# Gated linear recurrence and a two-layer network in one hand-ordered kernel: inputs loaded per unit, weights issued between them, old state added on the vector engine, output matmuls after the first silus

## The chip, the core and the metric

The kernel runs on one core of a Trainium2 chip. The core has a matrix engine (TensorE, here PE; PEld is its weight load), a vector engine (VectorE, DVE), an activation engine (ScalarE, ACT), a general engine (GpSimd, POOL), and SyncE (SP), which here only issues transfers. Sixteen DMA engines move the data. The metric is the device time of one execution in microseconds (µs), as the median of several runs.

## What is computed

A recurrence over 768 positions for 4 batches and 8 heads of 48 channels, followed by two matrix products with a silu between them:

```python
f = 1.0 / (1.0 + np.exp(-f_logit))
for t in range(S):
    state = f[:, :, t, :, None] * state + np.einsum('bhd,bhe->bhde', k[:, :, t], v[:, :, t])
    y[:, :, t] = np.einsum('bhd,bhde->bhe', q[:, :, t], state)
x = y.transpose(0, 2, 1, 3).reshape(B * S, H * D)      # 3072 x 384
h = x @ w_in                                            # 384 x 2048
out = (h * (1.0 / (1.0 + np.exp(-h)))) @ w_out          # 2048 x 384
```

The inputs q, k, v and f_logit are float32, 4.7 MB each; the weights are 3.1 MB each in float32 and are used in bfloat16.

## The kernel before

**Tiles and stages.** Positions are cut into 6 chunks of 128. A *unit* is one chunk of one batch (128 positions, 8 heads, 48 channels: 128x384), and a *half-chunk* `m` is two units, `m.0` and `m.1` (one chunk, two batches). There are 12 half-chunks and 24 units. Half-chunks m and m + 2 hold the same two batches, one chunk on, so the state goes from m to m + 2.

For each half-chunk the inputs `f`, `k`, `q`, `v` are loaded (`load`, SP), 128x768 float32 each. `logs` (ACT) makes log(1 + exp(-f)) in two instructions, `f_ld` and `lf`. Then for each unit:

- `cumsum` (cs, PE) sums the logs along the positions by a triangular matrix; `inverse` (ia) and `forward` (a) on ACT take their exponentials; `totals` and `decay_all` (al) give the decay of the whole chunk.
- `scale_k` (ki, POOL) and `scale_q` (qg, DVE) multiply k and q by them; `values` (vb, POOL, for half-chunk 1 on ACT) casts v.
- `transposes` (T, `t_ps`, PE) turns qg and ki, `transposed` (qk, DVE) copies them out of PSUM, `scores` (A, `a_ps`, PE) multiplies them, `masked` (am, `atm`, DVE) keeps the causal part in two instructions.
- `outputs` (Y, `y_ps`, PE) multiplies by v and, from half-chunk 2 on, adds the old state times q; `output_copy` (yc, DVE), `turn` (X, `x_ps`, PE) and `turned` (xT, DVE) make the network's input.
- `update` (D, `d_ps`, PE), in half-chunks 0 to 9, forms the new state; from half-chunk 2 on its first matmul multiplies the old state by the identity, so that it is summed in PSUM (L334). `state` (st, DVE) multiplies it by the decay.

For each half-chunk the network follows: eight steps I (`mlp_in`, six matmuls of 128x256 each, into `h_ps`), each with a silu S on ACT (`silu`, 128x512, into `hT`), then for each of the two batches four steps O (`mlp_out`, four matmuls of 128x384 each, into `o_ps`), a copy and a store (`result`, ACT, queue of ACT).

**What sets the order.** The order is written out by the program itself, before anything runs. `Plan` holds every step as a task with an engine, an assumed duration, needs, a rank and pools of buffers. `Plan.run` plays them through and notes when each would start; `emit` then issues the instructions in that order, and every engine works through its own part in exactly this order. `allowed` adds gates: steps I and O are not mixed except where the mode turns, ACT's table for exp and its table for silu are kept apart, and a step that opens an accumulator is held back while silus are pending. Until I0 starts, PE's waiting is filled with matmuls of zeros (`warm`, `w_ps`).

**Transfers.** Loads are issued on SP in the order f, k, q, v of half-chunk 0, then of 1. The weights are cast on the way, so they are issued on POOL, in eight pieces (four of `w_in` with 512 columns, four of `w_out` with four row blocks), all at once after ki of unit 1.1 (task `weights`). The loads of half-chunk 2 and later stand on SP behind a tiny transfer out of the sixth weight piece (`behind`, L477), so that they don't overtake the weights. The pool `ld` has four buffers for each input. In the built program all transfers of SP and ACT use eight landing counters in turn, in the order of issue, and one that takes a counter first waits for the last transfer on it.

Of the kernel before, what the change touches and what calls it, by code (L numbers as in the profile page):

```python
# [17 lines left out]
class Plan:  # L18
# [30 lines left out]
    def run(self, filler=None, until=None):  # L49
# [8 lines left out]
        self.silus = self.exps = turned = 0  # L58
        while left:
# [45 lines left out]
            if e == "PE" and kind in "IO":  # L105
                self.mode = kind
                if kind == "I" and t["name"].endswith(".0"):
                    self.silus += self.per_half
            if kind == "S":
                self.silus -= 1  # L110
# [17 lines left out]
    def allowed(self, cand, fronts, free):  # L128
# [4 lines left out]
        if kind in "IO" and t["engine"] == "PE":  # L133
            if kind == self.mode:
                return True
            now = [c for c in fronts.get("PE", ()) if c[2]["name"][0] == self.mode and c[0] <= start + 0.7]
            pending = self.mode == "I" and self.silus
            return not now and not pending and not (kind == "I" and self.exps)
        if t["opens"] > 0 and self.mode == "I" and self.silus:
            return False  # L140
        if t["table"] == "exp" and not t["opens"] and self.mode == "I" and self.silus:
            return False
        return True

# [6 lines left out]
def kernel(  # L151
# [24 lines left out]
    ld = ctx.enter_context(tc.tile_pool(name="ld", bufs=4))  # L176
# [9 lines left out]
    def load(m, name):  # L186

        g, b0 = m // 2, m % 2 * HB
        t = ld.tile([C, HB, H, D], F32, name=f"{name}_ld")
        loaded[m, name] = t  # L190
        src = SRC[name].rearrange("b h s d -> s (b h) d")[g * C:(g + 1) * C, b0 * H:(b0 + HB) * H]
        nc.sync.dma_start(out=t.rearrange("p b h d -> p (b h) d"), in_=src)  # L192
# [35 lines left out]
    def logs(m):  # L228
        act_table("exp")
        f = loaded[m, "f"]  # L230
        nc.scalar.activation(f, f, AF.Exp, scale=-1.0)  # L231
        nc.scalar.activation(lf[m % 4][:, :, :, 0:D], f, AF.Ln, bias=1.0)
# [17 lines left out]
    def scale_k(m, j):  # L250
        nc.gpsimd.tensor_mul(ki[m % 4][:, j, :, 0:D], loaded[m, "k"][:, j], ias[m, j])  # L251

    def scale_q(m, j):
        nc.vector.tensor_mul(qg[m % 4][:, j, :, 0:D], loaded[m, "q"][:, j], aas[m, j])  # L254

    def values(m, j):
        nc.gpsimd.tensor_copy(vb[m % 4][:, j], loaded[m, "v"][:, j])  # L257

    def values_act(m, j):
        nc.scalar.copy(vb[m % 4][:, j], loaded[m, "v"][:, j])  # L260
# [69 lines left out]
    def update(m, j):  # L330
        b = m % 2 * HB + j
        d_ps = yps.tile([128, NP, 2 * D], F32, name="d_ps", tag="yd")
        if m >= 2:
            nc.tensor.matmul(d_ps, ident, st[b], start=True, stop=False, skip_group_check=True)  # L334
        for p in range(NP):
            nc.tensor.matmul(d_ps[:, p, :], ki[m % 4][:, j, 2 * p:2 * p + 2, :], vb[m % 4][:, j, 2 * p:2 * p + 2],
                             start=(m < 2 and p == 0), stop=(p == NP - 1), skip_group_check=True)
        d[m, j] = d_ps

    def state(m, j):  # L340
        b = m % 2 * HB + j
        for r in range(2):
            lo = 64 * r
            nc.vector.tensor_mul(st[b][lo:lo + D, :, r * D:(r + 1) * D],  # L344
                                 d[m, j][lo:lo + D, :, r * D:(r + 1) * D],
# [56 lines left out]
    def loads(m):  # L402
        for name in "fkqv":
            needs = []
            if m >= 4:
                o = m - 4
                if name == "f":
                    needs = [f"L{o}"]
                else:
                    needs = [U({"k": "ki", "q": "qg", "v": "vb"}[name], o, j) for j in range(HB)]  # L410
            transfer(f"{name}{m}", 2.15 + 1.7 * (name + str(m) == "f0"), do(load, m, name), needs)
# [3 lines left out]
    for n in range(0, d_ff, 512):  # L415
        transfer(f"wi{n}", 2.05 + 1.0 * (n == 0), None, [])
# [5 lines left out]
    for m in range(NH):  # L422
        g = m // 2
        add(f"L{m}", "ACT", 1.7, do(logs, m), [f"f{m}"] + ([U("cs", m - 4, j) for j in range(HB)] + [f"al{m - 4}"] if m >= 4 else []),
            rank=m * 10 + 5, table="exp")
        add(f"al{m}", "PE", 0.2, do(totals, m), [f"L{m}"], rank=m * 10 + 9, takes="yd", opens=1)
# [97 lines left out]
```

## Time and profile before

| | |
|---|---|
| median of 4 runs | 211.31 µs (211.16 to 212.63) |
| the profiled execution | 211.16 µs, its span 209.4 µs, mean granted PE clock 0.975 |
| PE busy | 189.2 µs (90%), of it `h_ps` 70.2, `o_ps` 67.8, zeros 12.2 |
| ACT, DVE, POOL busy | 127.0, 99.4, 45.1 µs |
| loads on SP | 48 of 384 KB, 6.4 to 6.7 µs from issue to landing |
| weight pieces on POOL | 8 of 384 KB, `w_in` 7.6 and `w_out` 13.1 µs to landing |
| stores on ACT's queue | 24 of 192 KB, 3.4 µs to landing |

The span goes from the first to the last instruction; what lies around it belongs to the device time too. Where parts of a profile are quoted, a line of a group names line, engine, operation, output and inputs, sizes and count, then busy time and the mean of one instruction in ns. The chain of waits is followed back from the last instruction: each piece is what the next one waited for. Digits are tenths in 40 equal slices of the span. The groups that the steps below use most are these:

```profile
L353 PE MATMUL h_ps<-xT,w_in_sb 128*128 128x256 bf16 x576 | 70.2, 276 | 4.4 <-ACT hT L362 2.7
L368 PE MATMUL o_ps<-w_out_sb,hT 128*128 128x384 bf16 x384 | 67.8, 326 | 0.0
L297 DVE TENSOR_TENSOR atm<-a_ps,triu 128x512 bf16<-128x512 f32 x48 | 30.9, 686 | 4.5 <-PE a_ps L290 3.5
L251 POOL TENSOR_TENSOR ki<-k_ld,ia 128x384 bf16<-128x384 f32 x24 | 24.7, 1043 | 92.8 <-ACT ia L243 92.7
L254 DVE TENSOR_TENSOR qg<-q_ld,a 128x384 bf16<-128x384 f32 x24 | 19.1, 806 | 56.7 <-ACT a L248 49.7
L317 DVE CAST y<-y_ps 128x384 bf16<-128x384 f32 x24 | 13.3, 556 | 10.1 <-PE y_ps L310 9.7
L231 ACT ACTIVATE f_ld<-f_ld 128x768 f32<-128x768 f32 x12 | 10.1, 843 | 11.3 <-DMA f_ld<-in_f_logit_dram 7.0
L344 DVE TENSOR_TENSOR st<-d_ps,al 48x192 bf16<-48x192 f32 x40 | 14.0, 350 | 0.3
```

### The profile page before, as it was taken

Reading aid. Unit: us, or ns where it says so; the run is one execution under the profiler, and the core shown is the slowest. Engines: PE = TensorE matmul, PEld = TensorE weight load, DVE = VectorE, ACT = ScalarE, POOL = GpSimd, SP = SyncE. Lnnn points to the kernel's source line nnn. Section 1 sums busy time; section 2 is a strip of 40 time slices with the busy share of each in tenths; the row PEclk is TensorE's granted clock in tenths of the full one; section 3 lists DMA queues with packets and bytes.
Section 4 is the critical chain, followed back from the end, with each engine's and each line's share of the span. In section 5 each row is a group of like instructions: output and inputs, shape, how many; then the busy total and the mean of one; then the engine's idle time right before and its main releaser. Section 6 shows DMA issues by size and latency. Waiting matters only on the chain.

```text
span 209.4 us, 4687 instructions
## 1 busy us (share of the span) xinstructions
PE 189.2 (90%) x1957; PEld 139.6 (67%) x1957; DVE 99.4 (47%) x198; ACT 127.0 (61%) x220; POOL 45.1 (22%) x66
## 2 busy tenths in 40 slices
PE   7876899996389979959998999999999999999992
PEld 3544588663368658746677886678976778986651
DVE  3288840028348438302899712888307897200000
ACT  3534469471824986898957679817796227894111
POOL 4319600042401043004514101430006300000000
PEclk9997999999759999999999999999999999999999
DMA  7998999999999999999999800931001110000222
GB/s 133 187 187 123 167 198 202 193 246 211 216 191 181 186 203 226 189 166 187 242 180 248 129 3 5 258 83 41 0 0 41 38 49 29 3 0 3 75 75 75
DMA packets 106293, 27.04 MB, mean 129 GB/s; under 512 B 99616, under 2 KB 106272, under 8 KB 106272
## 3 DMA queue, kind: packets, MB, share of 16 engines
q1 hardware_dynamic: 99104, 18.88, 58.2%
q0 software_dynamic: 3712, 3.15, 9.8%
q10 hardware_dynamic: 3456, 4.72, 7.0%
q8 instruction: 15, 0.25, 0.5%
q14 instruction: 6, 0.05, 0.1%
HBM read 25.17 MB, written 4.72 MB: 143 GB/s over the span
## 4 chain that ended last, share of the span: by engine, by line
PE 63%; DMA 13%; ACT 7%; SPq 5%; DVE 5%; POOL 3%; issue 2%; ACTq 0%; DVEq 0%
PE h_ps L353 25%; PE o_ps L368 22%; DMA w_out_sb<-in_moe_w_out_dram 6%; SPq L192 5%; PE t_ps L278 4%; DMA k_ld<-in_k_dram 4%; DMA q_ld<-in_q_dram 3%; PE a_ps L290 3%; ACT L224 2%; PE y_ps L306 2%; PE y_ps L310 2%; ACT f_ld L231 2%; POOL w_in_sb L213 2%; PE cs L238 1%; PE x_ps L323 1%
## 5 line engine op out<-in xcount | busy, mean ns | idle before, releaser
L353 PE MATMUL h_ps<-xT,w_in_sb 128*128 128x256 bf16 x576 | 70.2, 276 | 4.4 <-ACT hT L362 2.7
L362 ACT ACTIVATE hT<-h_ps 128x512 bf16<-128x512 f32 x96 | 56.6, 597 | 24.0 <-PE h_ps L353 20.8
L368 PE MATMUL o_ps<-w_out_sb,hT 128*128 128x384 bf16 x384 | 67.8, 326 | 0.0
L353 PEld LDWEIGHTS <-w_in_sb 128*128 128x128 bf16 x576 | 54.8, 99 | 12.8 <-issue 4.0
L368 PEld LDWEIGHTS <-hT 128*128 128x128 bf16 x384 | 36.4, 98 | 21.8
L254 DVE TENSOR_TENSOR qg<-q_ld,a 128x384 bf16<-128x384 f32 x24 | 19.1, 806 | 56.7 <-ACT a L248 49.7
L251 POOL TENSOR_TENSOR ki<-k_ld,ia 128x384 bf16<-128x384 f32 x24 | 24.7, 1043 | 92.8 <-ACT ia L243 92.7
L297 DVE TENSOR_TENSOR atm<-a_ps,triu 128x512 bf16<-128x512 f32 x48 | 30.9, 686 | 4.5 <-PE a_ps L290 3.5
L374 ACT COPY o_sb<-o_ps 128x384 f32<-128x384 f32 x24 | 11.5, 478 | 30.3 <-PE o_ps L368 30.2
L224 ACT ACT_TABLE_LOAD x14 | 18.0, 1283 | 2.1 <-ACT o_sb L374 1.2
L283 DVE COPY qk<-t_ps 128x1024 bf16<-128x1024 bf16 x24 | 16.4, 684 | 5.1 <-PE t_ps L278 5.1
L317 DVE CAST y<-y_ps 128x384 bf16<-128x384 f32 x24 | 13.3, 556 | 10.1 <-PE y_ps L310 9.7
L257 POOL CAST vb<-v_ld 128x384 bf16<-128x384 f32 x22 | 11.9, 569 | 25.7 <-DMA v_ld<-in_v_dram 20.9
L231 ACT ACTIVATE f_ld<-f_ld 128x768 f32<-128x768 f32 x12 | 10.1, 843 | 11.3 <-DMA f_ld<-in_f_logit_dram 7.0
L243 ACT ACTIVATE ia<-cs 128x384 f32<-128x384 f32 x24 | 11.8, 492 | 5.3 <-PE cs L238 3.9
L344 DVE TENSOR_TENSOR st<-d_ps,al 48x192 bf16<-48x192 f32 x40 | 14.0, 350 | 0.3
L381 PE MATMUL w_ps<-zeros 128*128 128x384 bf16 x53 | 12.2, 380 | 1.1 <-DVE zeros L483 1.1
L310 PE MATMUL y_ps<-vb,atm 128*128 128x48 bf16 x192 | 11.9, 185 | 1.5 <-DVE atm L297 1.0
L310 PEld LDWEIGHTS <-atm 128*128 128x128 bf16 x192 | 10.0, 97 | 4.0 <-DVE atm L297 2.1
L248 ACT ACTIVATE a<-cs 128x384 f32<-128x384 f32 x24 | 11.8, 491 | 0.0
L278 PE MATMUL t_ps<-ident,qg 128*128 128x128 bf16 x96 | 9.8, 227 | 1.5 <-DVE qg L254 1.5
L306 PE MATMUL y_ps<-st,qk 128*128 128x96 bf16 x80 | 10.0, 206 | 1.1 <-DVE xT L328 0.7
(37 smaller groups left out, 134.8 us busy)
## 6 DMA issues: line engine op xcount, KB each, us to landing
f_ld<-in_f_logit_dram SPq DMA_DIRECT2D x12, 384.0 KB, 6.5
k_ld<-in_k_dram SPq DMA_DIRECT2D x12, 384.0 KB, 6.4
q_ld<-in_q_dram SPq DMA_DIRECT2D x12, 384.0 KB, 6.7
v_ld<-in_v_dram SPq DMA_DIRECT2D x12, 384.0 KB, 6.7
out_dram<-o_sb ACTq DMA_DIRECT2D x24, 192.0 KB, 3.4
w_in_sb<-in_moe_w_in_dram POOLq DMA_DIRECT2D x4, 384.0 KB, 7.6
w_out_sb<-in_moe_w_out_dram POOLq DMA_DIRECT2D x4, 384.0 KB, 13.1
behind<-w_out_sb SPq DMA_DIRECT2D x1, 0.1 KB, 4.2
```

Of the source, the lines that this page charges most:

```text
L224: nc.scalar.preload_act_table_set(tables[name])
L231: nc.scalar.activation(f, f, AF.Exp, scale=-1.0)
L251: nc.gpsimd.tensor_mul(ki[m % 4][:, j, :, 0:D], loaded[m, "k"][:, j], ias[m, j])
L254: nc.vector.tensor_mul(qg[m % 4][:, j, :, 0:D], loaded[m, "q"][:, j], aas[m, j])
L278: nc.tensor.transpose(t[:, i, p, :], src[m % 4][:, j, 2 * p:2 * p + 2, :], ident)
L283: nc.vector.tensor_copy(qkT[m, j], t_ps[m, j])
L297: nc.vector.tensor_mul(atm[m, j][:, r], att[m, j][:, r], triu[:, None, :].to_broadcast([C, NP, C]))
L306: nc.tensor.matmul(y_ps[:, 2 * p:2 * p + 2, :], qkT[m, j][:, 0, p, :], st[b][:, p, :], start=not opened, stop=False, skip_group_check=True)
L310: nc.tensor.matmul(y_ps[:, 2 * p + r, :], atm[m, j][:, r, p, :], vb[m % 4][:, j, 2 * p + r, :], start=not opened, stop=True, skip_group_ch ...
L353: nc.tensor.matmul(h_ps[:, i], w_in_sb[:, kk, (n + i) * 128:(n + i + 1) * 128], xT[m][:, kk].rearrange("p b c -> p (b c)"), start=(kk == 0 ...
L362: nc.scalar.activation(hT[m][:, n:n + 2, :], hs[m, n], AF.Silu)
L368: nc.tensor.matmul(os[m, j], hT[m][:, i, j * C:(j + 1) * C], w_out_sb[:, i, :], start=(i == 0), stop=(i == NT - 1))
```

## The change

Four things are changed together.

1. **Loads per unit.** Each load takes one unit (128x384, 192 KB) instead of a half-chunk; the order is f, k, q, v of unit m.0, then of m.1. The pool has eight buffers of half the size. The logs on ACT are made per unit as well, and a buffer comes free when one unit has used it.
2. **Weights between the loads.** The first weight piece is issued on POOL after vb of unit 0.1, the other seven after ki of unit 1.0, each a task of its own. `behind` needs the last piece's issue and the load of v of unit 1.1.
3. **Old state on DVE.** The matmul with the identity goes; from half-chunk 2 on, `state` first adds PSUM and the old state into a new tile `sd` (float32) and multiplies from there.
4. **Order of I, O and exp.** A step O needs the silus of its own four row blocks instead of all sixteen. PE may turn from I to O when all steps I of the half-chunk are issued, without its silus being done; exp work waits whenever silus are pending.

Assumed durations and ranks in the plan follow. The order that `Plan` writes out is therefore another one throughout.

```diff
@@ Plan.run @@
                 if kind == "I" and t["name"].endswith(".0"):
                     self.silus += self.per_half
+                    self.ins += self.per_half
+                self.ins -= kind == "I"
...
@@ Plan.allowed @@
-            now = [c for c in fronts.get("PE", ()) if c[2]["name"][0] == self.mode and c[0] <= start + 0.7]
-            pending = self.mode == "I" and self.silus
-            return not now and not pending and not (kind == "I" and self.exps)
-        if t["opens"] > 0 and self.mode == "I" and self.silus:
-            return False
-        if t["table"] == "exp" and not t["opens"] and self.mode == "I" and self.silus:
+            now = [c for c in fronts.get("PE", ()) if c[2]["name"][0] == self.mode and c[0] <= start + self.patience]
+            return not now and not (self.mode == "I" and self.ins) and not (kind == "I" and self.exps)
+        if (t["opens"] > 0 or t["table"] == "exp" and not t["opens"]) and self.silus:
             return False
...
-    ld = ctx.enter_context(tc.tile_pool(name="ld", bufs=4))
+    ld = ctx.enter_context(tc.tile_pool(name="ld", bufs=8))
...
-    def load(m, name):
+    def load(m, j, name):
...
-        t = ld.tile([C, HB, H, D], F32, name=f"{name}_ld")
+        t = ld.tile([C, H, D], F32, name=f"{name}_ld")
...
-    def logs(m):
+    def logs(m, j):
         act_table("exp")
-        f = loaded[m, "f"]
+        f = loaded[m, j, "f"]
         nc.scalar.activation(f, f, AF.Exp, scale=-1.0)
-        nc.scalar.activation(lf[m % 4][:, :, :, 0:D], f, AF.Ln, bias=1.0)
+        nc.scalar.activation(lf[m % 4][:, j, :, 0:D], f, AF.Ln, bias=1.0)
...
     def update(m, j):
-        b = m % 2 * HB + j
         d_ps = yps.tile([128, NP, 2 * D], F32, name="d_ps", tag="yd")
-        if m >= 2:
-            nc.tensor.matmul(d_ps, ident, st[b], start=True, stop=False, skip_group_check=True)
...
     def state(m, j):
         b = m % 2 * HB + j
+        src = d[m, j]
+        if m >= 2:
+            src = wk.tile([128, NP, 2 * D], F32, name="sd")
+            nc.vector.tensor_add(src, d[m, j], st[b])
...
-                                 d[m, j][lo:lo + D, :, r * D:(r + 1) * D],
+                                 src[lo:lo + D, :, r * D:(r + 1) * D],
...
     def loads(m):
-        for name in "fkqv":
...
+        for j in range(HB):
+            for name in "fkqv":
+                user = U({"f": "L", "k": "ki", "q": "qg", "v": "vb"}[name], m - 4, j)
+                first = (m, j, name) == (0, 0, "f")
+                transfer(U(name, m, j), 1.07 + 1.7 * first, do(load, m, j, name), [user] if m >= 4 else [])
...
                 add(f"O{m}.{j}.{n}", "PE", 0.655, do(mlp_out, m, j, n),
-                    [f"S{m}.{NT - 2}", f"wo{n}"] + ([f"O{m}.{j}.{n - 4}"] if n else []),
+                    [f"S{m}.{n + 2}", f"wo{n}"] + ([f"O{m}.{j}.{n - 4}"] if n else []),
...
-    add("weights", "POOL", 6.5, weights, [U("ki", 1, 1)], rank=-10)
+    pieces = [(load_w_in, n) for n in range(0, d_ff, 512)] + [(load_w_out, n) for n in range(0, NT, 4)]
+    before = U("vb", 0, 1)
+    for i, (fn, n) in enumerate(pieces):
+        if i == 1:
+            before = U("ki", 1, 0)
+        add(f"weights{i}", "POOL", 0.85, do(fn, n), [before], rank=-10 if i else 2.5)
+        before = f"weights{i}"
+
+
+    add("behind", "SP", 0.1, lambda: nc.sync.dma_start(out=behind, in_=w_out_sb[0:1, 4, 0:64]), [before, U("v", 1, 1)])
```

## The prediction

> **What bounds the kernel now.** I read the slices of the page first, then busy time by stage, then the chain of waits, then the DMA queues in short stretches. Times inside a run are µs from the span's start. The slices:
>
> ```profile
> PE   7876899996389979959998999999999999999992
> PEclk9997999999759999999999999999999999999999
> DMA  7998999999999999999999800931001110000222
> ```
>
> PE is the bound, but not evenly: DMA is full until about 115 µs, and PE has its holes only before that. The stages cut at I0 (23.3, first `h_ps` matmul of half-chunk 0), O0 (36.1), the end of O1 (47.7) and I2 (59.0) give their size; the columns are the stretch, its length, and the busy time of each engine:
>
> ```profile
> 23.30:36.10 12.80, 12.28 (x134) 10.64 (x135) 4.91 (x12) 8.74 (x15) 1.05 (x2) 1.00 1.25 194
> 36.10:47.70 11.60, 11.60 (x85) 6.98 (x82) 1.23 (x2) 6.81 (x13) 2.74 (x4) 1.00 1.16 221
> 47.70:59.00 11.30, 5.43 (x75) 3.79 (x75) 7.32 (x16) 5.16 (x9) 3.62 (x5) 0.84 1.15 209
> 59.00:76.00 17.00, 16.22 (x161) 11.99 (x160) 8.03 (x17) 10.76 (x17) 1.46 (x3) 0.90 1.27 187
> 76.00:95.00 19.00, 15.39 (x181) 12.83 (x178) 8.53 (x16) 15.39 (x25) 4.18 (x7) 1.00 1.23 195
> 95.00:112.00 17.00, 16.33 (x191) 11.17 (x190) 12.36 (x22) 12.71 (x25) 6.24 (x8) 1.00 1.23 211
> 112.00:206.00 94.00, 93.64 (x988) 71.50 (x985) 43.22 (x83) 56.97 (x102) 13.22 (x16) 1.00 0.24 56
> ```
>
> PE idles 5.9 µs at 47.7:59.0, then 0.8 + 3.6 + 0.7 = 5.1 up to 112, and 0.4 after it. So the end is the start of I0, plus PE's work, plus these holes: whatever moves I0 moves the end, unless a hole takes it up. The hole before I2 is the input of half-chunk 3, behind a store that waits on ACT (chain of waits):
>
> ```profile
> 44.19 7.83 DMA k_ld<-in_k_dram
> 52.10 0.34 ACTq L376
> 52.49 0.85 ACT f_ld L231
> ```
>
> What starts I0 is the first weight piece, issued on POOL at 18.1 and used at 23.3:
>
> ```profile
> 18.11 3.24 POOL L213 DMA_DIRECT2D w_in_sb<-in_moe_w_in_dram  x4
> 23.32 0.83 PE L353 MATMUL h_ps<-xT,w_in_sb 128*128 128x256 bf16 x6 [0.59 <-DMA w_in_sb<-in_moe_w_in_dram]
> ```
>
> Last, what a load gets beside another queue. Packets and MB by queue: alone (15:16), beside the last weight piece (36.3:37.0), beside stores (47.7:48.2 and 100.6:101.0). q1 are the loads, q0 the weights, q10 the stores:
>
> ```profile
> q1 hardware_dynamic: 976, 0.19, 145.2%
> ...
> q0 software_dynamic: 151, 0.11, 101.9%
> q1 hardware_dynamic: 179, 0.03, 24.0%
> ...
> q10 hardware_dynamic: 74, 0.11, 90.3%
> q1 hardware_dynamic: 55, 0.01, 10.9%
> ...
> q10 hardware_dynamic: 51, 0.08, 86.6%
> q1 hardware_dynamic: 54, 0.01, 18.7%
> ```
>
> Alone the loads move 976 packets (of 192 bytes) per µs. Beside a queue with long packets they fall to about one packet for each of the other's: 288 packets in 1.6 µs, 180 per µs. In the kernel before, the weights begin when the loads are through (40 load packets in 19.2:19.7, 53 of weights in 20.0:20.5), so they hardly meet.
>
> **The change, part by part.**
>
> *Loads per unit.* 96 of 192 KB for 48 of 384 KB. Half of a 2.05 issue (SP, L192) is 1.03, and 1,024 packets at 976 per µs are 1.05. Today f0 is seen by ACT at 4.75, so f0.0 at 3.7 and the n-th piece at 3.7 + 1.05 (n - 1): v0.1 (8th) 11.1, f1.0 12.1, k1.0 13.2, q1.0 14.2. SP's issues stand 0.04 apart, so 48 more cost at most 1.9 of SP, hidden under the holes. Exp and Ln of `f_ld` come in halves: 128x768 takes 843 ns, 128x384 (L243) 492, so 24 x (2 x 0.492 - 0.843) = 3.4 more on ACT, which is 15.39 of 19 busy at its fullest: bounds 0 and 3.4, taken 0.
>
> *Weights among the loads.* weights0 follows vb0.1 on POOL: 11.1 + 0.57 (L257) = 11.7; its packets flow 1.7 later, as 18.1 to 19.8 today. weights1 to 7 follow ki1.0: 12.1 + two halves on ACT 0.98 + cs 0.35 + ia 0.49 + ki 1.04 = 15.0, packets from 16.7. The other POOL work passed by the seven issues (about 0.8 each) is ki1.1, then not before 20.5; it waits longer for its load. At 16.7 unit 1.0 is loaded: from 13.4 on, weights0 (2.3 at 0.17 MB per µs, 20.5:21.5) squeezes v1.0 alone. Left are f1.1, k1.1, q1.1 and v1.1, beside three `w_in` pieces of 2.3 and four `w_out` pieces of 2.0 (0.20 MB per µs, 34:35): 14.9 of weights without a gap.
>
> What waits for q1.1? In the built program DVE has qg1.1 ahead of the atm of unit 1.0, and PE has y and d of unit 1.0 ahead of I0.0. In the kernel before, I0.0 stands ahead of y1.0. So I0 now waits for q1.1, by way of qg1.1, atm1.0 and y1.0, and with it all of I0 and I1 on PE and the y copy, state and xT of unit 1.0 on DVE. Three pieces are 3,072 packets; at 180 per µs 17.1, landing 33.8, seen about 1.0 later, 34.8. The weights end about there too, so it can't be much later. Then 0.56 (qg) + 1.29 (atm, two) + 0.36 (y) + 0.17 (d): **I0 at 37.2, 13.9 later**. Bounds of this term: at 256 per µs (36.3:37.0, where some engines were free of weights already) 12.0 in place of 17.1 gives +8.8; 110 per µs (47.7:48.2) is cut off by the end of the weights, about 36.2, which gives +15.3.
>
> The row above stands against a rule of the Trainium skill, "DMA: Bandwidth & Descriptors", sections "Queues, rings and completion order" and "SWDGE vs HWDGE vs iDMA": a DMA engine takes turns between its queues by whole packets of several descriptors, preferably up to 4,096 bytes. If turns were equal in bytes, the loads would keep about half their rate, and the sum would be that of the first rival; the stretches beside stores show far less than half.
>
> *What the holes take back.* With I0 at 37.2, I0 to O1 (12.3 + 11.6 of PE) end at 61. The loads of half-chunks 2 and 3 start near 35 as today (L477 waits for the same weight piece; today 34.6), so they have landed by then, and no store meets them on ACT; the chain over ACT, DVE and PE to I2 stays. Of the 5.9 I take two thirds, 3.9 (bounds 0 and 5.9).
>
> *O after the first silus, and the new gates.* O needs only the silu of its own pieces, and exp work waits for pending silus. The table loads stay 14 (L224, 1.28 each). What it can give is in the 5.1 of holes at 59:112: bounds 0 and 5.1, taken half, 2.5. The tail is PE's own (0.4 idle from 112 on; four O stages stand last instead of three), so nothing there.
>
> *Old state on DVE.* It removes 16 matmuls of 128x384 (L334). PE's price is that of the same shape in the tail, 96 in 15.61 (chain, L368): 16 x 0.163 = **2.6**. It adds 16 adds of 128x384 from PSUM on DVE: 0.56 each as L317 (bounds 0.35 as L328, 0.69 as L297), 8.9 in all. DVE is 99.4 of 209.4; the cover is thin at 95:112 (12.36 of 17). Taken 0, up to 8.9 if all shows.
>
> *Clock.* I2's first 12 matmuls take 2.72 today instead of 1.31: the clock was granted at half after the hole. A wait of ten µs at I0 should bring that 1.4 there, and it may vanish at I2; taken 0, bounds -1.4 and +1.4.
>
> Sum: 13.9 - 3.9 - 2.5 - 2.6 = +4.9 on the span of 209.4, 214.3. Around the span lie 211.16 - 209.4 = 1.8, so 216.1; that execution is 0.15 under the median of 211.31, so I say **216.2 µs**.
>
> **The rivals.**
>
> *Loads keep half their rate; faster.* q1.1 then takes 3,072 / 488 = 6.3 after 16.7, seen at 24.0, I0 at 26.4, +3.1. The hole before I2 takes a part of it, since I2 is then set by a store on ACT: the built program uses eight landing counters in turn for SP and ACT, a transfer waits for the last one on its counter, and the first store of O1 so waits for k3.1, the 14th piece after 36.5: 36.5 + 14.7 + 2.7 (three stores, 192 KB each at 0.11 MB in 0.5) + 1.0 = 54.9. From there the store's issue, al, ia, a, qg, T, qk, A, atm, y, its copy, x and xT (6.6 by their rows) lead to I2 at 61.5, +2.5 against 59.0. With -2.3 (14 matmuls left) and -2.5: -2.3, **209.0**. For it: in 36.8:37.1 the loads had 195 packets beside 44 of the last weight piece, as engines came free of it. Against: both stretches beside stores. It decides as soon as loads keep more than some 400 packets per µs.
>
> *The same, but the holes at 59:112 stay:* +2.5 - 2.3 = +0.2, **211.5**. For it: the table loads are as many as before.
>
> *DVE becomes the bound:* half rate, and every second add on the path, 8 x 0.56 = 4.5: -2.3 + 4.5 = +2.2, **213.5**. For it: DVE is 8.83 of 10 busy at 100:110. Against: the next reader of a state is two half-chunks on.
>
> **How the numbers follow.** About 0.5% (1.1 µs) is what a measurement of this kernel can tell from no change. Starved loads 0.57, own range 212 to 219.5 (from the rate of the loads and the holes); half rate and faster 0.24 (207 to 210.3); even 0.12; DVE 0.07. Slower than 212.4: 0.54 + 0.06 + 0.02 = 0.62. Faster than 210.2: 0.25. The rest, 0.13, within. Range 208.5 to 219: it leaves out the lower part of the faster case (0.11) and the top of the first (0.06).
>
> **What would show it.** Right: in the profile after, packets of q1 near 180 per µs at 18:30; `qg` of unit 1.1 on DVE waiting for `q_ld` until 30 or later; I0 at 32 to 38 with PE idle or in warm matmuls before it; a half-clock slice there; no L334 with identity, 16 adds near 0.56. Wrong: I0 before 28, or I2 before 62. Then the loads share well, and the end follows the first two rivals.

## The result, and the profile after

The changed kernel takes 212.85 µs (median of 40 runs, 211.38 to 217.92) where the kernel before takes 212.12 µs in the same sessions (66 runs). The ratio is 1.0039, with an interval of 1.0024 to 1.0054: slower by 0.2 to 0.5%. Ratios here and below leave out the runs that took over 1.5% longer than the fastest of the same kernel. The forecast was 216.2 µs, 4.9 above the run before; measured is about 0.8. The sign held, the size did not, and the sign held in part by luck, as the wait that counts was not the one forecast; by the 0.5% set in the prediction the two kernels are equal.

The profiled execution has a span of 210.7 µs (before 209.4) at a mean granted clock of 0.968. Its slices:

```profile
PE   7878197999579999997999899999989999999992
PEclk9999769999958999999999999999999999999999
DMA  7999999999899999999993995000111000002222
```

PE has a 1 in the fifth slice (21 to 26 µs) where it had an 8 before, and near 53 to 63 a 5 and a 7 where it had a 3 and an 8. The stages, cut at I0 (26.8), O0 (41.9), the end of O1 (53.9) and I2 (64.0); the columns are as in the prediction (stretch, length, busy PE, PEld, DVE, ACT and POOL, clock, DMA share, GB/s):

```profile
26.80:41.90 15.10, 13.84 (x134) 11.86 (x132) 5.03 (x11) 10.25 (x17) 0.50 (x1) 0.88 1.12 186
41.90:53.90 12.00, 12.00 (x93) 7.20 (x90) 1.77 (x2) 6.87 (x15) 1.00 (x1) 1.00 1.04 188
53.90:64.00 10.10, 6.04 (x74) 4.22 (x74) 9.25 (x18) 4.16 (x10) 3.28 (x5) 0.69 1.23 217
64.00:80.00 16.00, 15.11 (x172) 11.12 (x169) 10.60 (x20) 13.17 (x26) 5.39 (x7) 0.98 1.14 194
80.00:112.00 32.00, 30.73 (x366) 24.91 (x361) 20.29 (x39) 24.89 (x43) 6.72 (x10) 1.00 1.14 201
```

Set beside the kernel before, stage by stage, with the terms of the prediction:

| stretch | before | after | difference | forecast |
|---|---|---|---|---|
| start to I0 | 23.3 | 26.9 | +3.6 | +13.9 |
| I0 to O0 | 12.9 | 15.1 | +2.2 | 0 |
| O0 to I2 | 22.8 | 21.9 | -0.9 | -3.9 |
| I2 to the last matmul of O | 146.3 | 142.7 | -3.6 | -5.1 |
| sum | | | +1.3 | +4.9 |

**What held I0.** The wait was foreseen at the right place: `qg` of unit 1.1 on DVE waits for `q_ld`, and atm and y of unit 1.0, which PE needs ahead of I0, stand behind it. The timeline of DVE (start, duration, instruction, in brackets the idle time before it and what ended it):

```profile
24.47 0.56 DVE L255 TENSOR_TENSOR qg<-q_ld,a 128x384 bf16<-128x384 f32 x1 [5.38 <-DMA q_ld<-in_q_dram]
```

But it ends at 24.5, not at 34.8. The DMA queues of the changed kernel in three stretches, 17:18, 18:20 and 24:30 (q0 weights, q1 loads; packets, MB, time of the packets as a share of the stretch), tell why:

```profile
q0 software_dynamic: 146, 0.15, 87.1%
q1 hardware_dynamic: 154, 0.03, 26.4%
...
q1 hardware_dynamic: 1801, 0.34, 87.9%
q0 software_dynamic: 129, 0.12, 34.7%
...
q0 software_dynamic: 1449, 1.19, 124.8%
q1 hardware_dynamic: 124, 0.02, 3.5%
```

Beside the first weight piece the loads fall to one packet for a packet of weights, 154 per µs (forecast 180). Then comes a gap: in 18:20 the weights have only 129 packets, and the loads move 1,801. By 20.0 they have moved 15,999 of the 16,640 packets of all loads up to v1.1. POOL's timeline shows when the pieces were issued:

```profile
12.91 0.93 POOL L214 DMA_DIRECT2D w_in_sb<-in_moe_w_in_dram  x1
14.89 0.99 POOL L252 TENSOR_TENSOR ki<-k_ld,ia 128x384 bf16<-128x384 f32 x1 [1.05 <-ACT ia L244]
15.84 2.34 POOL L214 DMA_DIRECT2D w_in_sb<-in_moe_w_in_dram  x3
```

The second piece is issued at 15.84 (forecast 15.0), yet its packets flow in strength only from 20, some 4 µs later and not 1.7. The reason is open. In part it may stand behind the first piece, whose packets are through only at about 19.6; but in g1 (below), where the second piece is issued at 15.3, the weights move nothing at all from 18.2 to 18.6, with the first piece through.

**What held the silus.** What the weights did hold up is v1.1, the last load. Its vb is on ACT, and the first silus stand behind it; the prediction had not named this waiter. O0 comes 11.5 after the start of this vb, and so it does in e6 and f2 below (36.3 to 47.8, 30.8 to 42.3), with I0 at 26.9, 33.6 and 27.3. So in these kernels O0 is set by v1.1 and not by I0. ACT's timeline:

```profile
30.44 0.51 ACT L261 CAST vb<-v_ld 128x384 bf16<-128x384 f32 x1 [10.89 <-DMA v_ld<-in_v_dram]
30.97 1.28 ACT L225 ACT_TABLE_LOAD   x1
32.27 2.10 ACT L364 ACTIVATE hT<-h_ps 128x512 bf16<-128x512 f32 x4
...
50.78 0.48 ACT L376 COPY o_sb<-o_ps 128x384 f32<-128x384 f32 x1 [0.62 <-PE o_ps L370]
53.02 0.34 ACTq L378 DMA_DIRECT2D out_dram<-o_sb  x1
53.41 0.18 ACT L273 ACTIVATE al<-al_ps 128x8 f32<-128x8 f32 x1 [2.15 <-PE a_ps L291]
```

The last three lines show the second thing that counts below. The copy `o_sb` is done at 51.3, but its store is issued at 53.0, and al, ia and a stand behind it. The releaser named at `al` (PE) doesn't explain it, since the store stands ahead of al and needs only the copy; the chain of waits says what it was, and what that load had waited for:

```profile
18.95 13.87 DMA w_out_sb<-in_moe_w_out_dram
...
46.69 6.26 DMA k_ld<-in_k_dram
```

That is the wait for the landing counter, on a load of half-chunk 3, and this load stands on SP behind the weights. Neither I0 nor O0 lies on this chain. This store is issued only 0.9 later than the one that waits in the kernel before (53.0 and 52.1), but from there to I2 it is 10.9 instead of 6.9. The difference is as large as DVE's part: its steps make up 4.9 of this stretch of the chain (before 0.9), and it is busy for 9.25 of the last 10.1 before I2 (before 7.32 of 11.3). The add is 0.5 of the 4.9; what the new order puts there was not tried.

**Parts that moved as costed.** Groups of the changed kernel: the adds on DVE, the state from them, and the halved exp:

```profile
L343 DVE TENSOR_TENSOR sd<-d_ps,st 128x384 f32<-128x384 f32 x16 | 8.8, 547 | 0.3 <-PE d_ps L334 0.3
L346 DVE TENSOR_TENSOR st<-sd,al 48x192 bf16<-48x192 f32 x32 | 12.6, 394 | 0.8
L232 ACT ACTIVATE f_ld<-f_ld 128x384 f32<-128x384 f32 x24 | 12.5, 520 | 5.0 <-DMA f_ld<-in_f_logit_dram 3.7 <-ACT o_sb L376 1.2
```

The add takes 547 ns (forecast 0.56); the state after it 394 instead of 350; the exp 520 (492). DVE goes from 99.4 to 110.0 µs busy.

### The profile page after: what moved, and what is told of

Read it like the earlier page. It is cut to its first block, busy times and chain, and to the rows that moved or that the text cites. A ratio compares the mean times of both kernels' runs of the same rounds, so it can differ in the third digit from the quotient of the medians.

```text
span 210.7 us, 4752 instructions
## 1 busy us (share of the span) xinstructions
PE 188.2 (89%) x1938; PEld 137.7 (65%) x1938; DVE 110.0 (52%) x214; ACT 130.6 (62%) x244; POOL 45.7 (22%) x66
## 4 chain that ended last, share of the span: by engine, by line
PE 54%; DMA 12%; ACT 10%; DVE 10%; SPq 6%; issue 4%; POOL 2%; ACTq 1%; DVEq 0%
PE h_ps L355 24%; PE o_ps L370 15%; DMA w_out_sb<-in_moe_w_out_dram 7%; SPq L193 6%; PE t_ps L279 3%; DVE qg L255 3%; DMA k_ld<-in_k_dram 3%; PE w_ps L383 3%; PE a_ps L291 2%; ACT L225 2%; DMA f_ld<-in_f_logit_dram 2%; DVE atm L298 2%; PE x_ps L324 2%; ACT a L249 2%; DVE qk L284 2%
## 5 line engine op out<-in xcount | busy, mean ns | idle before, releaser
L355 PE MATMUL h_ps<-xT,w_in_sb 128*128 128x256 bf16 x576 | 71.3, 276 | 1.8 <-ACT hT L364 1.8
L370 PE MATMUL o_ps<-w_out_sb,hT 128*128 128x384 bf16 x384 | 67.6, 326 | 0.0
L364 ACT ACTIVATE hT<-h_ps 128x512 bf16<-128x512 f32 x96 | 56.0, 597 | 17.0 <-PE h_ps L355 14.2
L255 DVE TENSOR_TENSOR qg<-q_ld,a 128x384 bf16<-128x384 f32 x24 | 19.6, 821 | 42.6 <-ACT a L249 37.1
L244 ACT ACTIVATE ia<-cs 128x384 f32<-128x384 f32 x24 | 11.7, 488 | 15.1 <-PE cs L239 13.4
L311 PE MATMUL y_ps<-vb,atm 128*128 128x48 bf16 x192 | 12.7, 187 | 7.1 <-DVE atm L298 7.1
L258 POOL CAST vb<-v_ld 128x384 bf16<-128x384 f32 x22 | 13.3, 625 | 19.7 <-DMA v_ld<-in_v_dram 18.5
L311 PEld LDWEIGHTS <-atm 128*128 128x128 bf16 x192 | 10.2, 98 | 10.7 <-DVE atm L298 10.1
L232 ACT ACTIVATE f_ld<-f_ld 128x384 f32<-128x384 f32 x24 | 12.5, 520 | 5.0 <-DMA f_ld<-in_f_logit_dram 3.7
L346 DVE TENSOR_TENSOR st<-sd,al 48x192 bf16<-48x192 f32 x32 | 12.6, 394 | 0.8
L233 ACT ACTIVATE lf<-f_ld 128x384 bf16<-128x384 f32 x24 | 12.6, 523 | 0.8
```

Of the source, the lines that this page charges most:

```text
L255: nc.vector.tensor_mul(qg[m % 4][:, j, :, 0:D], loaded[m, j, "q"], aas[m, j])
L311: nc.tensor.matmul(y_ps[:, 2 * p + r, :], atm[m, j][:, r, p, :], vb[m % 4][:, j, 2 * p + r, :], start=not opened, stop=True, skip_group_ch ...
L355: nc.tensor.matmul(h_ps[:, i], w_in_sb[:, kk, (n + i) * 128:(n + i + 1) * 128], xT[m][:, kk].rearrange("p b c -> p (b c)"), start=(kk == 0 ...
L364: nc.scalar.activation(hT[m][:, n:n + 2, :], hs[m, n], AF.Silu)
L370: nc.tensor.matmul(os[m, j], hT[m][:, i, j * C:(j + 1) * C], w_out_sb[:, i, :], start=(i == 0), stop=(i == NT - 1))
```

## The experiments

Ratios are to the kernel before in the same session, with 95% intervals. Landings of loads and the stretches at half clock are read from the packets and the granted clock in the traces. A profile shows one execution, and executions of one kernel differ in the granted clock: of f1's twelve runs, those at a mean of 0.967 take 210.9 to 211.6 µs, those at 0.975 209.6 to 210.4, the one at 0.983 208.65. So a difference between two profiles holds some of that too.

**One part undone, one part alone**

e1: all weights where they stood before, the other three parts kept.

```diff
-        add(f"weights{i}", "POOL", 0.85, do(fn, n), [before], rank=-10 if i else 2.5)
...
+    add("weights", "POOL", 6.5, weights, [U("ki", 1, 1)], rank=-10)
```

> The changed kernel with one part undone: all eight weight pieces are issued after ki of unit 1.1 again, as before the change. Theory (weights among the loads hold back q1.1 and v1.1, and with them DVE, ACT's silus and PE): v1.1 lands near 19 and not at 29.9, I0 starts at 23 to 24 and O0 at 36 to 37 (41.97 in the changed kernel), I2 near 60 (63.9), the end 3 to 5 earlier than the changed kernel: 208 to 210. Rival (the loads per unit are the cost, by the store on ACT that waits for a landing counter before I2): I2 stays at 62 or later and the time within 1 of the changed kernel, 212 to 214.

Measured: 210.83 µs, ratio 0.9953 (0.9919 to 0.9987). In its profile I0 stands at 24.8, O0 at 38.1, I2 at 61.2, and the last matmul of O at 203.9. The gain is less than the theory's, but the rival's marks (I2 at 62 or later, 212 to 214) were not met either. The weights' part, with the order that the plan wrote for it, is the one that costs: 1.0039 against 0.9953. From I2 on both take the same 142.7. I0 is still 1.5 later than before the change: with loads per unit ki of unit 1.1 is done later, and the first weight piece is issued at 19.5 instead of 18.1.

e2: the kernel before with the old state added on DVE (part 3 alone).

```diff
-            nc.tensor.matmul(d_ps, ident, st[b], start=True, stop=False, skip_group_check=True)
...
+            nc.vector.tensor_add(src, d[m, j], st[b])
```

> The kernel before with one part alone: old state added on DVE. Theory: 16 identity matmuls go from PE (2.6), the adds of about 0.56 lie beside other work: 209 to 211. Rival (DVE is full in the attention stages and PE waits for the adds): 213 to 217.

Measured: 211.34 µs, 0.9974 (0.9947 to 1.0001). The gain is 0 to 1.1 µs, where the 16 matmuls were priced at 2.6.

e3: the kernel before with the new gates and needs of O (part 4 alone).

```diff
-            pending = self.mode == "I" and self.silus
-            return not now and not pending and not (kind == "I" and self.exps)
+            return not now and not (self.mode == "I" and self.ins) and not (kind == "I" and self.exps)
...
-                    [f"S{m}.{NT - 2}", f"wo{n}"] + ([f"O{m}.{j}.{n - 4}"] if n else []),
+                    [f"S{m}.{n + 2}", f"wo{n}"] + ([f"O{m}.{j}.{n - 4}"] if n else []),
```

> The kernel before with one part alone: output matmuls after the first silus, and the new gates. Theory: half of the holes of PE at 59:112 (5.1) go: 209 to 211. Rival (the number of table loads stays 14, the holes move and do not go): 211.5 to 213.

Measured: 210.52 µs, 0.9940 (0.9916 to 0.9964), so -1.3 where -2.5 was taken (bounds 0 and -5.1).

e4: the kernel before with loads and logs per unit (part 1 alone, weights as before).

```diff
-    def load(m, name):
+    def load(m, j, name):
...
```

> The kernel before with one part alone: loads and logs per unit, the weights after ki of unit 1.1 as before. Theory: the first units start 1 earlier, the weights too by up to 1, ACT is 3.4 longer in the sum: 210 to 212.5. Rival (stores on ACT now meet loads of half the size and wait for their counters, I2 2 later or more): 213 to 216.

Measured: 211.14 µs, 0.9961 (0.9931 to 0.9990). Taken was 0; it is a small gain, although I0 comes at 25.4, 2.1 later than before. So three parts gain a little each, 0.3 to 0.6% (e2's interval just reaches no change), and the three together (e1) gain no more than one of them.

**What the weights among the loads do**

e5: vb of unit 1.1 on POOL, so that ACT doesn't wait for v1.1.

```diff
-            on_act = m == 1
+            on_act = (m, j) == (1, 0)
```

> The changed kernel with vb of unit 1.1 on POOL in place of ACT; nothing else is edited. In the changed kernel ACT stands at that vb from 19.6 to 30.4 (10.9 us, v_ld), and the first silus stand behind it. Theory: this wait, not the one for q1.1, is what the weights among the loads cost: the silus start at about 27.5, O0 comes from 42.0 to 38 or 39, I2 from 63.9 to about 61.5, and the time falls by 1 to 2 us, to a ratio of about 0.997 to the kernel before. Rival: the stage before I2 takes the gain up (its loads and stores stand where they stood), or v1.1 now holds POOL and ki of half-chunk 2 behind it: I2 stays at 63 to 64.5 and the ratio at 1.004.

Measured: 213.46 µs, 1.0089 (1.0053 to 1.0124). The first half of the theory held: O0 moved from 42.0 to 37.1. The rest fell, and the time is no shorter. The rival put I2 at 63 to 64.5; it came at 62.8. ACT now meets the loads with its stores. Its timeline in e5:

```profile
40.57 0.48 ACT L376 COPY o_sb<-o_ps 128x384 f32<-128x384 f32 x1 [0.27 <-PE o_ps L370]
44.79 0.37 ACTq L378 DMA_DIRECT2D out_dram<-o_sb  x1
45.20 0.48 ACT L376 COPY o_sb<-o_ps 128x384 f32<-128x384 f32 x1 [4.16 <-DMA v_ld<-in_v_dram]
47.44 0.34 ACTq L378 DMA_DIRECT2D out_dram<-o_sb  x1
47.88 0.49 ACT L244 ACTIVATE ia<-cs 128x384 f32<-128x384 f32 x1 [2.19 <-DMA k_ld<-in_k_dram]
```

The first store stands ready at 41.0 and is issued at 44.8, the second waits 1.8, and so on: each for a load on its landing counter. O1 ends at 54.7, later than the 53.9 of the changed kernel. Of the 4.9 gained at O0, 1.1 are left at I2. After I2 the clock stands at half until 67.6 (change 64.5), and the first O of half-chunk 2 comes 9.5 after I2 instead of 7.5; in this profile that takes more than the 1.1.

e6: the changed kernel without the gap: weights1 to 7 follow weights0 at once.

```diff
-        if i == 1:
-            before = U("ki", 1, 0)
```

> The changed kernel with weights1 to 7 directly behind weights0 on POOL, without the wait for ki of unit 1.0; ki of units 1.0 and 1.1 stand behind all eight. Theory: the starvation is as the prediction took it (one load packet for a packet of weights, 180 per us), and only the gap in the weights at 18 to 20 kept it from f1.1, k1.1 and q1.1. Without the gap the weights flow from about 14.5 to 31, q1.1 lands at 30 to 33, qg of unit 1.1 waits on DVE until then, I0 stands at 33 to 36, and the time is 214 to 218. Rival: the loads get through all the same, since the share is not that small over a longer stretch: q1.1 lands before 24, I0 before 29, time 211 to 213.5.

Measured: 216.79 µs, 1.023 (1.0181 to 1.0278). The theory held for the load and for I0. The DMA queues of e6 at 16:17, 20:24 and 24:30, and its DVE line:

```profile
q0 software_dynamic: 172, 0.18, 114.6%
q1 hardware_dynamic: 8, 0.00, 1.4%
...
q0 software_dynamic: 653, 0.64, 94.0%
q1 hardware_dynamic: 653, 0.12, 27.8%
...
q0 software_dynamic: 1127, 0.90, 93.4%
q1 hardware_dynamic: 1127, 0.21, 32.3%
```

```profile
31.06 0.56 DVE L255 TENSOR_TENSOR qg<-q_ld,a 128x384 bf16<-128x384 f32 x1 [12.60 <-DMA q_ld<-in_q_dram]
```

From 20 on it is one packet for one packet, 163 and 188 per µs; at 16:17 the loads get even less, 8 to 172, though q1.1 was issued at 13.9 and hasn't landed. `qg` of unit 1.1 runs at 31.1, I0 at 33.6, O0 at 47.8, I2 at 67.8. So the starvation that the prediction had described for the changed kernel comes when the weights flow on, and the gap kept the changed kernel from it. Two things qualify this. The plan writes another order here too: T of unit 1.1, and not y of unit 1.0, stands ahead of I0, but I0 still waits for q1.1. And the time, nearly that of the prediction, isn't reached by its path. The chain of waits goes by the last load to its vb on ACT at 36.3, the silus and O0:

```profile
15.04 21.21 DMA v_ld<-in_v_dram
```

(The profiled execution took 218.68 µs, 1.9 above the median.)

e7: the first piece early as in the change, the other seven after ki of unit 1.1.

```diff
-            before = U("ki", 1, 0)
+            before = U("ki", 1, 1)
```

> The changed kernel with the first weight piece after vb of unit 0.1 as it is, and the other seven after ki of unit 1.1 as in the kernel before. Theory: one piece among the loads costs them some 2.5 us at most, which v1.0 to q1.1 take up before they are needed; the other seven no longer meet them. v1.1 lands at about 20 to 22, I0 at 24 to 26, O0 at 38 to 39, time as with all weights back, ratio 0.993 to 0.998. Rival: any piece among the loads costs what all of them cost, ratio 1.002 or more.

Measured: 212.43 µs, 1.0025 (0.9999 to 1.0052). The landmarks came as expected up to O0 (I0 24.0, O0 37.6), the time didn't: as in e5 the early stores wait on ACT (3.3 µs from the end of the second copy, 43.7, to the issue of its store at 47.1), O1 ends at 52.9 and I2 stands at 61.9, 0.7 later than in e1. Another 1.9 come after I2, where the clock stands at half until 67.1 (e1 62.2). The theory fell where it went from O0 to the time. The rival's ratio was met, but not its reason: up to O0 this kernel is as early as e1.

**The store that waits**

e8: e1, with the four stores of half-chunks 0 and 1 on POOL's queue. f1: the same in the kernel before. f2: the same in the changed kernel. One line in each:

```diff
-        nc.scalar.dma_start(out=out[r0:r0 + C, :], in_=o_sb)
+        (nc.gpsimd if m < 2 else nc.scalar).dma_start(out=out[r0:r0 + C, :], in_=o_sb)
```

> The changed kernel with all weights after ki of unit 1.1 (as in the first experiment), and the four stores of half-chunks 0 and 1 issued on POOL's queue in place of ACT's. In the first experiment ACT stands before the second and third store's issue for 2.6 and 0.4 us, since a transfer waits for the last one on its landing counter, a load of half-chunk 3. Theory: this wait sets I2: without it ia and a of half-chunk 2 and 3 come 2 to 3 us earlier, I2 comes from 61.2 to 59 or 60, and the time falls by about 1 us, ratio 0.988 to 0.992. Rival: the loads of half-chunk 3 themselves set it (the last lands at about 52 to 56), or the stores on POOL hold ki: I2 stays at 61 and the ratio at 0.995 or above.

Measured: 208.65 µs, 0.9866 (0.9824 to 0.9907), and I2 at 58.5. The same stretch of ACT in e1, then in e8:

```profile
46.92 0.48 ACT L376 COPY o_sb<-o_ps 128x384 f32<-128x384 f32 x1
50.00 0.34 ACTq L378 DMA_DIRECT2D out_dram<-o_sb  x1
50.44 0.49 ACT L244 ACTIVATE ia<-cs 128x384 f32<-128x384 f32 x1 [3.04 <-PE a_ps L291]
```

```profile
46.95 0.48 ACT L376 COPY o_sb<-o_ps 128x384 f32<-128x384 f32 x1 [0.70 <-PE o_ps L370]
47.82 0.49 ACT L244 ACTIVATE ia<-cs 128x384 f32<-128x384 f32 x1 [0.39 <-PE cs L239]
```

The copy runs at the same time in both; ia behind it comes 2.6 µs earlier, and I2 2.7 (61.2 to 58.5).

> The kernel before with the four stores of half-chunks 0 and 1 issued on POOL's queue in place of ACT's, nothing else. In its profile ACT stands from 48.2 to 52.1 before the third store's issue, until k of half-chunk 3 has landed, and f_ld and lf of that half-chunk stand behind it. Theory: this wait is most of the hole before I2 (5.9 us of PE); without it I2 comes from 59.0 to 55 to 57 and the time falls by 2 to 3.5 us, ratio 0.984 to 0.992. Rival: the stores on POOL gave the last experiment its gain only together with loads per unit (half a load lands earlier), since here q3 and v3 land at 52.6 and 55.1 anyway: I2 at 58 to 59, ratio 0.995 to 1.0.

Measured: 210.35 µs, 0.9921 (0.9891 to 0.9952), I2 at 56.8. I2 moved as expected (the store that waits in the kernel before, issued at 52.1, is the fourth and not the third); the gain of 1.7 µs is a little under the expected 2 to 3.5. From I2 to the last matmul of O this kernel takes 148.5 in its profile (before 146.3), with the clock at half for 5.3 µs after I2 (3.3) and once more at 89.4 to 92.8.

> The changed kernel with the same four stores on POOL's queue, the weights among the loads as they are. Theory: what the weights' place costs (1.0086 against the kernel with all weights back) comes from v1.1 on ACT, I0 to O0 being 2 to 4 us late; without the wait on ACT before I2 this delay comes through to I2 in full: I2 at 62, time 210.5 to 212.5, ratio 0.994 to 1.004, so 2 to 3 us above the kernel with the weights back and the stores on POOL (208.65). Rival: the store wait is what made the delay count; without it both places of the weights give the same, 208 to 209.5.

Measured: 211.41 µs, 0.9965 (0.9923 to 1.0008), I2 at 62.4: 2.8 above e8, as the theory had it. Between the two the weights' place costs 1.0% (0.9965 to 0.9866); with the wait it was 0.86% (1.0039 to 0.9953). So the two losses are separate, and the rival falls: taking the wait away does not make the weights' place free. Weights' place here means the transfers and the order that the plan wrote for them, together. I2 says the same: 63.9 with both, 62.4 without the wait, 61.2 without the weights among the loads, 58.5 without either. With the wait gone, v1.1 on ACT, the silus and O0 are the chain to I2.

f3: e8 with the stores of half-chunks 0 to 5 on POOL.

```diff
-        (nc.gpsimd if m < 2 else nc.scalar).dma_start(out=out[r0:r0 + C, :], in_=o_sb)
+        (nc.gpsimd if m < 6 else nc.scalar).dma_start(out=out[r0:r0 + C, :], in_=o_sb)
```

> Weights back and stores of half-chunks 0 to 5 on POOL's queue (12 of 24). Theory: only the stores of half-chunks 0 and 1 stand in front of work that sets a hole; the later ones meet loads too, but PE has hardly a hole after I4, so the time is that of four stores on POOL, 208 to 209.2. Rival: the holes at 68 to 95 (3.3 us of PE in all) have the same cause, and the time falls by another 1 us or more, below 207.8.

Measured: 211.13 µs, 0.9952 (0.9919 to 0.9985). Both expectations fell: it is 2.5 slower than e8. POOL's timeline in f3:

```profile
72.92 0.58 POOL L378 DMA_DIRECT2D out_dram<-o_sb  x1 [6.18 <-ACT o_sb L376]
73.51 1.96 POOL L252 TENSOR_TENSOR ki<-k_ld,ia 128x384 bf16<-128x384 f32 x2
```

A store waits for its copy on POOL too, and ki stands behind it (again at 91.2): the wait has only changed its engine. I of half-chunk 3 comes at 78.2 (e8: 77.0).

f4: e8 with the old state on PE as before (loads per unit, new gates, four stores on POOL).

```diff
-            nc.vector.tensor_add(src, d[m, j], st[b])
...
+            nc.tensor.matmul(d_ps, ident, st[b], start=True, stop=False, skip_group_check=True)
```

> Loads per unit and the new gates, the old state added on PE as before, weights as before, four stores on POOL's queue. Against the run with four stores on POOL (208.65) this undoes the add on DVE alone. Theory: the add is worth the 16 matmuls (2.6 us of PE) less what the longer DVE chain costs in the stages before 112; the runs so far put it at 0.5 us alone: 208.5 to 210. Rival: DVE is the limit in the holes at 70 to 112, and without the adds it is faster: below 208.2.

Measured: 208.51 µs, 0.9831 (0.9779 to 0.9882), against 0.9866 (0.9824 to 0.9907) with the adds: the intervals overlap, so the adds' worth can't be told from nothing here.

f5: the kernel before with the new gates and four stores on POOL; loads per half-chunk, weights and old state as before. Its diff is that of e3 and that of e8.

> The kernel before with the new gates and four stores on POOL's queue: loads per half-chunk, weights as before, the old state on PE. Theory: the gains of the gates (0.9940 alone) and of the stores (0.9921 alone) take away different holes and add up, 0.984 to 0.988, and loads per unit add little (0.9831 with them). Rival: both take the same hole before I2, 0.990 to 0.994.

Measured: 208.00 µs, **0.9811 (0.9783 to 0.9839)**, the lowest median of all, 3.7 µs below the kernel before in its session, with two small edits. Its six runs go from 207.2 to 212.2. From f4 it can't be told apart, so loads per unit add nothing that shows. The gains of e3 (0.9940) and f1 (0.9921) add up (their product is 0.9861), so they don't take away the same hole. Two of its stages (end of O1 to I2, and 92.5 to 112):

```profile
47.20:56.80 9.60, 5.34 (x77) 3.35 (x76) 7.84 (x16) 5.16 (x9) 4.64 (x7) 0.95 1.15 213
92.50:112.00 19.50, 19.50 (x255) 17.17 (x252) 12.38 (x27) 13.73 (x24) 4.60 (x8) 1.00 1.15 192
```

The hole before I2 is 4.3 (5.9 before), and from 92.5 to 112 PE doesn't idle.

**Transfers or order?** Since the weights are tasks in the plan, moving them also has the plan write another order: in the changed kernel `T` of unit 1.1 comes after the first matmuls of I0 on PE, in e1 ahead of y of unit 1.0. g1 has e1's order with the weights issued as in the change; g2 the change's order with all eight pieces after ki of unit 1.1. The issues are hung on the steps in front of them, here for g1, whose first piece stands in `values` for unit 0.1 in the same way; in g2 the condition is (1, 1), and all eight pieces and `behind` follow:

```diff
     def scale_k(m, j):
         nc.gpsimd.tensor_mul(ki[m % 4][:, j, :, 0:D], loaded[m, j, "k"], ias[m, j])
+        if (m, j) == (1, 0):
+            for n in range(512, d_ff, 512):
+                load_w_in(n)
+            for n in range(0, NT, 4):
+                load_w_out(n)
```

> The weights are issued where the changed kernel issues them (the first piece after vb of unit 0.1, seven after ki of unit 1.0), but PE, DVE and ACT work in the order of the first experiment, whose plan still has the weights as one task after ki of unit 1.1. Theory: the transfers are the cost, as f1.1 to v1.1 meet the weights; the first silus stand behind v1.1 on ACT in this order too: O0 at 40 to 42, I2 at 62.5 to 64, ratio 1.001 to 1.006. Rival: the order is the cost (y and d of unit 1.0 and T of unit 1.1 ahead of I0 on PE): then I0 at 22 to 24, I2 at 60 to 61.5, ratio 0.992 to 0.998.

Measured: 215.12 µs, 1.016 (1.0131 to 1.0190). I0 is at 24.6, as early as in e1, yet O0 is at 41.9 and I2 at 63.7, as in the changed kernel: the late I0 is not what the weights cost, the late v1.1 is. But the time is 2.3 above the changed kernel's, more than the theory allowed. In its profile this lies behind I2: the first O of half-chunk 2 comes 9.9 after I2 instead of 7.5, with the clock at half until 69.4 (change: until 64.5).

> The changed kernel's order on PE, DVE and ACT, with all eight weight pieces issued after ki of unit 1.1 as before. Theory (transfers): unit 1.1 lands at 19.5, I0 waits for the first piece at 24.5, O0 at 38, I2 at 61, ratio 0.993 to 0.998. Rival (order): ratio 1.001 to 1.006 as in the changed kernel.

Measured: 212.97 µs, 1.0036 (1.0009 to 1.0063). The rival held, against my theory: with the transfers alone put back the time stays that of the change. O0 is 3.6 earlier (38.4), but the loads of half-chunk 2 begin at 38.1 instead of 34.6, and the third store (the first of half-chunk 1) is issued at 51.1 after 3 µs of waiting; I2 comes at 62.0, the last O ends 0.6 earlier.

So the two don't add: in e1's order the transfers' place costs 2% (0.9953 to 1.016), in the change's order nothing (1.0036 to 1.0039). At I2 this is not so: there the transfers' place costs 2.5 in e1's order and 1.9 in the change's, and the order 0.8 and 0.2. What makes the sums differ lies behind I2:

| run | I2 | clock at half until | first O of half-chunk 2 | from I2 to it |
|---|---|---|---|---|
| change | 63.9 | 64.5 | 71.5 | 7.5 |
| e1 | 61.2 | 62.2 | 68.9 | 7.7 |
| g1 | 63.7 | 69.4 | 73.6 | 9.9 |
| g2 | 62.0 | 65.3 | 70.8 | 8.8 |
| e8 | 58.5 | 63.0 | 67.8 | 9.4 |
| f2 | 62.4 | 62.7 | 69.8 | 7.4 |

All six have the same 48 matmuls of I there; the longer the clock stays at half behind I2, the longer the stage. So an earlier I2 can lose most of its gain again: g2 has I2 1.9 earlier than the change and loses 1.2 of it here. Each row is one execution, so how much of it belongs to the kernel and how much to the execution is open, and with it the reason why the two don't add. Which step of the order costs the 0.8% between e1 and g2 was not tried.

## Why the prediction was wrong

*Loads per unit, 0.* e4 gives -0.4%, somewhat better than taken. The second exp and ln cost 2.4 of busy time on f_ld where 1.7 was worked out (24 x 0.520 less 10.1), and didn't show in the time. What did move is I0: 25.4 in e4, 2.1 later, as the weights wait for a later ki of unit 1.1. The prediction had no term for that.

*Weights among the loads, +13.9: here it failed,* in its start and in its path. The start: the step as written is "weights1 to 7 follow ki1.0: 12.1 + ... = 15.0, packets from 16.7", and from there "14.9 of weights without a gap" (which by these two figures end at 31.6, not at the 33.8 or 36.2 that its sum and its upper bound take). The issue was only 0.8 late, but the stream came at 20, because the time from issue to packets, 1.7 in the row of the kernel before, was 2.5 for the first piece and about 4 for the next. By then f1.1, k1.1 and nearly all of q1.1 had gone, at nearly the full rate (825 and 976 per µs at 18:19 and 19:20). I0 moved by 3.6, and 1.5 of that stand in e1 too, where the weights are back; the weights' own part is 2.1. The rate (180 per µs; measured 154 to 188, for a time far less in e6), the waiter (qg of unit 1.1, ahead of atm and y of unit 1.0) and the price of the steps behind it (2.4 forecast and measured) were right: e6, where the stream begins at about 14.8 and hardly pauses, shows I0 at 33.6.

The path: even a late I0 is not what the weights cost. O0 follows vb of unit 1.1 on ACT, 11.5 after it in the change, in e6 and in f2, and g1 has I0 at 24.6 and O0 at 41.9 all the same. So e6's 216.8 µs, close to the 216.2 of the forecast, are reached by v1.1 and not by q1.1; that the two numbers are close is partly luck. The prediction hung the largest term on a race of 3 µs between two queues, took the starting time from one row at its face value, and gave bounds for the rate alone, none for the start.

*Missing, +2.2 from I0 to O0:* v1.1 on ACT with the silus behind it. The prediction listed what waits for q1.1 and stopped there; the load after it had a waiter on another engine. In the changed kernel itself the chain to I2 goes by the store that waits; where no store waits, the late O0 shows in full (I2 at 62.4 in f2, 58.5 in e8).

*Holes, -3.9.* O0 to I2 gave back 0.9. The prediction reasoned that with I0 at 37 no store would meet a load; as I0 came at 27, they met. The first rival's mechanism was at work in this stage: the store on ACT that waits for its landing counter. It put I2 at 61.5; 63.9 was measured. e8, f1 and f2 show what the wait is worth, 0.7 to 0.9%, 1.6 to 1.8 µs. It isn't the whole: the rival took 6.6 from the store to I2, by rows of the kernel before, and 10.9 were measured, 4.9 of them on DVE. That goes the way of the third rival, though DVE holds one stage here and not every second add.

*Order of I and O, -2.5, and old state, -2.6.* Alone they are worth 1.3 and 0 to 1.1 (e3, e2). In the profiles the time from I2 on falls by 3.6, not 5.1. Not all of that is theirs: the clock stood at half for 3.3 µs after I2 in the run before and for 0.6 in the run after, which is about half of the difference of 2.7, 1.4, by itself. That the 16 matmuls are worth 2.6 is not shown; f4 can't tell the adds from nothing.

*Clock, 0.* It was in its bounds, and as the last point shows not 0 in the profiled pair. The half clock at I0 came as foreseen (23.6 to 30.4); the one at I2 didn't vanish.

The rivals' times were 209.0, 211.5 and 213.5. The measured time lies between two of them, but none describes it: beside the weights the loads did not keep half their rate, they got through in a gap. "Wrong: I0 before 28" was the sign set in the prediction, and it came true.

## What to carry to other kernels

When one queue can starve another, the outcome hangs on who has finished when the other begins: bound the starting time by every row that shows issue to first packet, and list the waiter of each transfer still open at that moment, on every engine: the last one to land may set the stage. A store issued from a working engine's queue can wait for an unrelated load by way of a shared landing counter; the sign is a finished copy, a late issue, and work behind it that no releaser explains. Moving an early stage is worth only what the next wait lets through: take that wait away first, then the earlier moves begin to count. And before a small gain is read off two profiles, the granted clock in both should be looked at.

## What the runs showed of the hardware

- Over stretches of 4 and 6 µs with both queues open, the DMA engines gave the loads and the weights one packet each: 653 to 653 and 1,127 to 1,127 in e6. In bytes the second is 0.21 to 0.90 MB. It isn't a floor: at 16:17 of e6 it was 8 to 172; why was not tried. The Trainium skill ("DMA: Bandwidth & Descriptors", "Queues, rings and completion order") has the engines take turns by packets, which the counts of the two stretches bear out; so the rows don't stand against that rule, as the prediction had put it: as the load's packets hold 192 bytes, equal turns are far from equal shares.
- A load beside weights was seen some 3 µs after its count of packets was through. In e1, without weights beside it, the last of the 16,640 packets is through by 19.5 and ACT uses `v_ld` of unit 1.1 at 19.9. In e6 as many packets as the loads up to q1.1 hold (15,600) are through at 28.0, and DVE sees q1.1 at 31.1. The counts don't say which load a packet belongs to, so whether the signal is late or the last packets of q1.1 are isn't shown.
- From issue on POOL to the first packets of a weight piece: 1.7 µs in the kernel before and 1.5 in e1, with the loads through; 2.5 in the change, with loads flowing; for the second piece there about 4.
- PE's clock went to half in stretches of 3.4 µs or a multiple of it (before 17.9 to 21.3 and 55.5 to 62.3, after 23.6 to 30.4 and 57.7 to 64.5). How far such a stretch reaches behind I2 ran from none (f4) to 5.7 µs (g1). The skill ("TensorE: Matmul & The Clock Gate", "Part 1: The HAM clock gate") has a free-running window of about that length; the runs agree with the length.
